# Retention, then two expert layers: the loads of retention in another order and four at a time, rows of the first tiles kept back, a wide product in halves

## The chip, the cores and the metric

One core of a Trainium2 chip. The core has five engines that run side by side: TensorE (PE, matrix products; PEld is its loading of weights), VectorE (DVE), ScalarE (ACT), GpSimd (POOL) and SyncE (SP), whose queue issues most transfers. The metric is the time of one execution on the device in microseconds (us); lower is better. The kernel before takes 798.01 us, the median of 3 runs (797.87 to 800.58).

## The reference

```python
def _attn_ref(q, k, v):                       # 4 x 8 heads x 576 x 64
    scores = scale * np.matmul(q, k.transpose(0, 1, 3, 2))
    gamma = 1.0 - 2.0 ** (-5.0 - np.arange(H))
    Dmat = np.where(rel >= 0, gamma ** rel, 0.0)
    return np.matmul(scores * Dmat, v)
def _moe_ref(x, w_gate, w1, w2):              # 2304 tokens, 8 experts, 288 tokens each
    logits = x @ w_gate                       # the largest logits are served first, greedily
    ...
    out[mask] = np.maximum(x[mask] @ w1[e], 0.0) @ w2[e]
def _moe2_ref(x, w_in, w_out):                # 512 -> 2048 -> 512
    h = x @ w_in
    return (h * np.tanh(softplus(h))) @ w_out
```

Retention (attention with a decay in place of the softmax) makes x of 2304 tokens by 512; each token is assigned to one of 8 experts, and a gated layer follows. All is in float32.

## The kernel before, in words

Only the first part, `attention`, is touched. It walks over 18 tiles of 128 tokens (all 8 heads at once). A sequence has 576 tokens, so a new one starts with tiles 0 and 9, and tiles 4 and 13 straddle two. One iteration t of the loop does this:

- `load(t + 3)`: two transfers of 512 KB on SP's queue, `qk` (queries and keys, transposed) and `kv` (keys and values). Each has five buffers.
- `scale(t + 3)` on GpSimd: `ks`, keys by their decay (needs `kv`), and then `qs`, queries by their decay (needs `qk`).
- `scores(t + 1)`: keys by queries on PE into `pA`; VectorE multiplies with a mask into `am`.
- `carried(t)`: the state of the tiles before by `qs` into `pT` (not in tiles 0 and 9).
- `outputs(t)`: `am` by values, into `pT` too; ScalarE copies it to `xT`.
- `state(t)`: `ks` by values into `pS`, and VectorE makes the next state `S` (not in tiles 8 and 17).
- `turn(t - 1)`: the wide product `pX`, `xT` by an identity with the gate's weights beside it. It turns the tile to rows and gives the gate's logits. VectorE reduces the logits into `L`, ScalarE copies the rows to `xs`, and SP stores them to `x_scratch`, 256 KB a tile, from where the experts gather them later.

PE, VectorE and GpSimd run in the order in which the code is written. ScalarE and SP get their order from a scheduler with a timeline of its own, so a transfer may stand in SP's queue elsewhere than in the code. SP issues in the order of its queue: a row that waits holds back all that stand behind it. In the kernel before, a transfer waits for the one eight places ahead (there are eight semaphores for transfers) and for its buffer. Four constant loads serve the routing that follows: `ident`, `tri`, `rc` and `ic`.

After tile 17 the routing starts on VectorE: `choices(early)` takes the logits of tiles 0 to 15, and it stands on VectorE behind the reduction of tile 16. A long chain of small VectorE and PE operations follows, and after it the experts, whose order on all engines comes from a planner that starts its own clock there.

Of the kernel before, what the change touches and what calls it, by code (L numbers as in the profile page):

```python
# [7 lines left out]
F32 = mybir.dt.float32  # L8
# [9 lines left out]
P = 128  # L18
B, H, S, D = 4, 8, 576, 64
N = B * S  # L20
DM = H * D
E = 8
# [3 lines left out]
NT = N // P  # L26
HP = H // 2
WARM = 11
STRADDLE = (4, 13)

GB = 96
# [42 lines left out]
def _layout(spec):  # L74
    out, o = {}, 0
    for name, n in spec:
        out[name] = slice(o, o + n)
        o += n
    return out, o


DC, DCN = _layout([("gk", NT * H), ("gs", NT * HP), ("gq", HP * P)])
# [45 lines left out]
class Kernel:  # L128
# [3 lines left out]
    def attention(self):  # L132
        tc, nc, a = self.tc, self.nc, self.a
# [7 lines left out]
        with ExitStack() as st:  # L141
            ld = st.enter_context(tc.tile_pool(name="ld", bufs=5))
            wk = st.enter_context(tc.tile_pool(name="wk", bufs=3))
# [3 lines left out]
            dec = one.tile([P, DCN], F32, name="dec")  # L147
# [3 lines left out]
            masks = [one.tile([P, 2, HP, P], F32, name=f"mask{i}") for i in range(2)]  # L151
            both = one.tile([P, 2, P + 2 * E], F32, name="both")
# [3 lines left out]
            QZ = {}  # L156
            for t in STRADDLE:
                QZ[t] = one.tile([P, HP, P], F32, name=f"qz{t}")
                nc.gpsimd.memset(QZ[t][:, :, 64:], 0.0)
            pS = ps.tile([P, HP, D], F32, name="pS")  # L160
            QK, KV, QS, KS, AM, XT, PT, seen = {}, {}, {}, {}, {}, {}, {}, [0]

            def load(t):

                if t < NT:
                    QK[t] = ld.tile([P, 2, HP, P], F32, name="qk")
                    nc.sync.dma_start(QK[t].rearrange("p a h i -> p (a h i)"), a["qk"][:, t])
                    KV[t] = ld.tile([P, 2, H, D], F32, name="kv")
                    nc.sync.dma_start(KV[t].rearrange("p a h d -> p (a h d)"), a["kv"][:, t])

            def starts(t):
                return (t * P) % S == 0

            def scale(t, eng):

                if t >= NT:
                    return
                if not starts(t + 1):
                    KS[t] = wk.tile([P, H, D], F32, name="ks")
                    eng.tensor_tensor(KS[t], KV[t][:, 0], gks[:, t, :, None].to_broadcast([P, H, D]), op=ALU.mult)  # L180
                if not starts(t):
                    n = 64 if t in STRADDLE else P
                    QS[t] = QZ[t] if t in STRADDLE else wk.tile([P, HP, P], F32, name="qs")
                    eng.tensor_tensor(QS[t][:, :, :n], QK[t][:, 0, :, :n], gqs.rearrange("p (h i) -> p h i", i=P)[:, :, :n], op=ALU.mult)

            def scores(t):
                if t >= NT:
                    return
                pA = [ps.tile([P, HP, P], F32, name=f"pA{i}", tag="pA", bufs=2) for i in range(2)]
                for hp in range(HP):  # L190
                    for i in range(2):
                        sl = slice(i * 64, i * 64 + 64)
                        for o in (slice(0, 64), slice(64, P)):
                            nc.tensor.matmul(pA[i][o, hp, :], QK[t][sl, 1, hp, o], QK[t][sl, 0, hp, :], start=True, stop=True)
                AM[t] = wk.tile([P, 2, HP, P], F32, name="am")
                for i in range(2):
                    nc.vector.tensor_tensor(AM[t][:, i], pA[i], masks[t in STRADDLE][:, i], op=ALU.mult)

            def state(t):

                if starts(t + 1):
                    return
                s1 = ((t + 1) * P - 1) % S
                begin = s1 < P
                lo = P - 1 - s1 if begin else 0
                for h in range(H):
                    o = slice(h % 2 * 64, h % 2 * 64 + 64)
                    nc.tensor.matmul(pS[o, h // 2, :], KS[t][lo:, h, :], KV[t][lo:, 1, h, :],
                                     start=(begin and h < 2), stop=False, skip_group_check=True)
                seen[0] += 1  # L210
                nc.vector.tensor_tensor(Sb[seen[0] % 2], pS, gss[:, t + 1, :, None].to_broadcast([P, HP, D]), op=ALU.mult)
# [25 lines left out]
            def turn(t):  # L237

                if t < 0:
                    return  # L240
                xs = wk.tile([P, DM], F32, name="xs")
                pX = ps.tile([P, 2, 512], F32, name="pX", tag="pT", bufs=2)
                for i in range(2):
                    for k in range(2):
                        nc.tensor.matmul(pX[:, i, k * P:k * P + P + E], XT[t][:, 2 * i + k, :], both[:, i, E - k * E:P + 2 * E - k * E],
                                         start=(k == 0), stop=(k == 1), skip_group_check=True)
                nc.vector.tensor_reduce(L[:, t, :], pX[:, :, P:P + E].rearrange("p i e -> p e i"), AX.X, ALU.add)
                for i in range(2):
                    nc.scalar.copy(xs.rearrange("p (k q i d) -> p i k q d", q=2, i=2, d=D)[:, i],
                                   pX[:, i, :2 * P + 2 * E].rearrange("p (k c) -> p k c", k=2)[:, :, :P].rearrange("p k (q d) -> p k q d", d=D))  # L250
                nc.sync.dma_start(a["x"][t * P:(t + 1) * P, :], xs)

            warm = one.tile([P, 512], BF16, name="warm")
            nc.vector.memset(warm, 0.0)
            nc.scalar.activation(warm[:, :1], warm[:, :1], AF.Sigmoid)
            nc.vector.memset(warm[:, :1], 0.0)
            pW = ps.tile([P, 2, 512], F32, name="pW", tag="pT", bufs=2)[:, 0]
            for _ in range(WARM):
                nc.tensor.matmul(pW, warm[:, :P], warm, start=True, stop=True)
            self.routing_setup()  # L260
            load(0)
            nc.sync.dma_start(masks[0].rearrange("p a h i -> p (a h i)"), a["masks"][:, 0])
            nc.sync.dma_start(dec, a["decays"])
            load(1)
            nc.sync.dma_start(both.rearrange("p i c -> p (i c)"), a["both"])
            nc.sync.dma_start(self.ident, a["ident"])
            self.tri = one.tile([P, P], F32, name="tri")
            nc.sync.dma_start(self.tri, a["tri"])
            load(2)
            nc.sync.dma_start(masks[1].rearrange("p a h i -> p (a h i)"), a["masks"][:, 1])  # L270
            scores(0)
            scale(0, nc.vector)
            scale(1, nc.gpsimd)
            scale(2, nc.gpsimd)
            for t in range(NT - 1):
                load(t + 3)
                scale(t + 3, nc.gpsimd)
                scores(t + 1)
                carried(t, Sb[seen[0] % 2])
                outputs(t)  # L280
                state(t)
                turn(t - 1)
                if t == 6:
                    self.routing_consts()
            t = NT - 1
            carried(t, Sb[seen[0] % 2])
            outputs(t)
            turn(t - 1)
            self.psum = lambda name, shape: ps.tile(shape, F32, name=name, tag="pS" if name == "pF" else "pA", bufs=1 if name == "pF" else 2)
            G = self.marks_of()  # L290
            self.chosen = self.rw.tile([GB, E, 3], I32, name="chosen", bufs=1)
# [2 lines left out]
            choice = self.choices(early)  # L294
            self.reached(choice, G, early)
            turn(t)
            self.choices(late, choice)
            self.reached(choice, G, late)
            for i in range(NT):
# [30 lines left out]
        nc.gpsimd.memset(self.ohb[:, NT * GB:], 0.0)  # L330
        self.tok = pr.tile([P, NT], I32, name="tok")

    def routing_consts(self):
        nc, a, pr = self.nc, self.a, self.persist
        rc = self.rc = pr.tile([P, RCN], F32, name="rc")
        nc.sync.dma_start(rc, a["rconsts"])
        self.ic = pr.tile([P, ICN], U32, name="ic")
        nc.sync.dma_start(self.ic, a["iconsts"])
        nc.vector.tensor_scalar(self.at("ic", U32), self.ic, self.ic[:, IC["all"]], None, op0=ALU.bitwise_and)
        self.before = pr.tile([P, P], BF16, name="before")  # L340
        nc.vector.tensor_tensor(self.before, self.tri, self.ident, op=ALU.subtract)
# [777 lines left out]
```

## Time and profile before

| | |
|---|---|
| median of 3 runs | 798.01 us |
| profiled execution | 803.52 us |
| its span, first to last instruction | 801.7 us |
| PE busy | 756.9 us (94%) |
| DVE busy | 664.2 us (83%) |
| granted TensorE clock, mean | 0.977 |
| moved by the DMA engines | 112.53 MB |

A line of the timeline gives start, duration, engine, source line, operation, output <- inputs and shape, and in brackets how long the engine was idle before and what ended that. x16 says that 16 records are merged. A line of stages gives the busy time of each engine in a stretch, then the granted clock, the busy share of the DMA engines and what they moved. Names end in a buffer number in the program, which is left out.

### The profile page before, as it was taken

Reading aid. Unit: us, or ns where it says so; the run is one execution under the profiler, and the core shown is the slowest. Engines: PE = TensorE matmul, PEld = TensorE weight load, DVE = VectorE, ACT = ScalarE, POOL = GpSimd, SP = SyncE. Lnnn points to the kernel's source line nnn. Section 1 sums busy time; section 2 is a strip of 40 time slices with the busy share of each in tenths; the row PEclk is TensorE's granted clock in tenths of the full one; section 3 lists DMA queues with packets and bytes.
Section 4 is the critical chain, followed back from the end, with each engine's and each line's share of the span. In section 5 each row is a group of like instructions: output and inputs, shape, how many; then the busy total and the mean of one; then the engine's idle time right before and its main releaser. Section 6 shows DMA issues by size and latency. Waiting matters only on the chain.

```text
span 801.7 us, 16170 instructions
## 1 busy us (share of the span) xinstructions
PE 756.9 (94%) x6184; PEld 682.4 (85%) x6184; DVE 664.2 (83%) x1080; ACT 412.7 (51%) x781; POOL 470.5 (59%) x407
## 2 busy tenths in 40 slices
PE   7999479999999999898999899999999999999996
PEld 5898338898998989798989789888998899889985
DVE  2444687888888888778799999989998998998993
ACT  1233115556565565756844465555546555555452
POOL 4643035779797897430376676666557566555544
PEclk9999779999999999899999999999999999999999
DMA  9994166889788887988300010010001001000001
GB/s 341 409 352 141 41 193 209 252 284 300 247 300 278 273 298 245 334 287 287 114 11 11 21 39 21 20 40 20 2 20 50 11 20 40 20 1 27 14 1 39
DMA packets 61261, 112.53 MB, mean 140 GB/s; under 512 B 4864, under 2 KB 33152, under 8 KB 61184
## 3 DMA queue, kind: packets, MB, share of 16 engines
q1 hardware_dynamic: 44960, 74.01, 27.3%
q10 hardware_dynamic: 13248, 28.06, 9.8%
q0 software_dynamic: 2976, 9.44, 3.6%
q8 instruction: 48, 0.79, 0.4%
q14 instruction: 29, 0.24, 0.1%
HBM read 88.94 MB, written 22.54 MB: 139 GB/s over the span
## 4 chain that ended last, share of the span: by engine, by line
PE 48%; DVE 10%; issue 4%; DMA 3%; POOL 2%; ACT 2%; ACTq 0%; SPq 0%; POOLq 0%; DVEq 0%
PE mmc L996 20%; PE po L1057 18%; PE mma L776 6%; DVE q L1026 4%; PE mmb L776 4%; DVE n L1021 2%; DMA st<-w 2%; DVE n L1031 1%; DMA st<-w_out 1%; POOL n L1028 1%; POOL gl L1038 1%; DVE G L433 1%; DVE words L742 1%; ACT whi L563 1%; DVE wlo L566 0%
## 5 line engine op out<-in xcount | busy, mean ns | idle before, releaser
L1026 DVE RECIPROCAL q<-q 128x384 f32<-128x384 f32 x96 | 244.3, 2545 | 13.5 <-ACT q L1017 7.4
L1028 POOL TENSOR_TENSOR n<-n,q 128x384 f32<-128x384 f32 x96 | 99.9, 1040 | 133.6 <-DVE q L1026 130.3
L1038 POOL TENSOR_TENSOR gl<-n,gh 128x384 fp32r<-128x384 f32 x96 | 104.4, 1088 | 56.8 <-ACT gh L1036 56.2
L996 PE MATMUL mmc<-yl,whi 128*128 128x384 f32 x384 | 130.2, 339 | 3.9 <-POOL yl L956 2.1
L996 PE MATMUL mmc<-yh,whi 128*128 128x384 f32 x384 | 130.7, 340 | 1.0 <-ACT yh L953 1.0
L996 PE MATMUL mmc<-yh,wlo 128*128 128x384 f32 x384 | 129.8, 338 | 0.0
L566 POOL TENSOR_TENSOR wlo<-st,whi 128x1024 fp32r<-128x1024 f32 x50 | 120.0, 2417 | 14.3 <-ACT whi L563 9.3
L1057 PE MATMUL po<-wlo,gh 128*128 128x512 f32 x288 | 115.6, 401 | 0.0
L1057 PE MATMUL po<-whi,gh 128*128 128x512 f32 x288 | 114.8, 399 | 0.0
L1057 PE MATMUL po<-whi,gl 128*128 128x512 f32 x288 | 114.0, 396 | 0.0
L1014 ACT ACTIVATE s<-mmc 128x384 f32<-128x384 f32 x96 | 47.2, 491 | 125.3 <-PE mmc L996 122.1
L1021 DVE SCALAR_TENSOR_TENSOR n<-s 128x384 f32<-128x384 f32 x96 | 102.0, 1062 | 3.1 <-ACT s L1014 1.2
L563 ACT CAST whi<-st 128x1024 fp32r<-128x1024 f32 x80 | 83.1, 1045 | 38.7 <-DMA st<-w 28.7
L776 PE MATMUL mma<-xh,whi 128*128 128x288 f32 x256 | 78.5, 307 | 3.4 <-ACT xh L623 2.7
L996 PEld LDWEIGHTS mmc<-yl,whi 128*128 128x128 f32 x384 | 72.1, 188 | 9.3 <-POOL yl L956 3.1
L776 PE MATMUL mma<-xl,whi 128*128 128x288 f32 x256 | 77.4, 302 | 1.7 <-DVE xl L625 1.7
L996 PEld LDWEIGHTS mmc<-yh,whi 128*128 128x128 f32 x384 | 72.2, 188 | 6.3 <-ACT yh L953 1.9
L776 PE MATMUL mmb<-hl,whi 128*128 128x288 f32 x256 | 77.3, 302 | 0.0
L776 PE MATMUL mmb<-hh,whi 128*128 128x288 f32 x256 | 77.2, 302 | 0.0
L776 PE MATMUL mma<-xh,wlo 128*128 128x288 f32 x256 | 76.9, 300 | 0.0
L776 PE MATMUL mmb<-hh,wlo 128*128 128x288 f32 x256 | 75.9, 297 | 0.0
L996 PEld LDWEIGHTS mmc<-yh,wlo 128*128 128x128 f32 x384 | 72.0, 187 | 0.0
(149 smaller groups left out, 1533.2 us busy)
## 6 DMA issues: line engine op xcount, KB each, us to landing
st<-w SPq DMA_DIRECT2D x64, 512.0 KB
qk<-qk SPq DMA_DIRECT2D x18, 512.0 KB
kv<-kv SPq DMA_DIRECT2D x18, 512.0 KB
std<-w_out ACTq DMA_DIRECT2D x15, 512.0 KB
std<-w_in ACTq DMA_DIRECT2D x14, 512.0 KB
x_scratch<-xs SPq DMA_DIRECT2D x18, 256.0 KB
y_scratch<-y ACTq DMA_DIRECT2D x32, 144.0 KB
yt<-y_scratch SPq DMA_DIRECT2D x22, 192.0 KB
```

The lines of the kernel that those rows point to most:

```text
L433: v.tensor_tensor(G[:, :NT * 64].rearrange("p (t m) -> p t m", m=64)[:, :, :m], key[:, :, None].to_broadcast([P, NT, m]), T[:, None, :].to ...
L563: self.nc.scalar.copy(dst[0], st)
L566: (self.nc.vector if lo.engine == DVE else self.nc.gpsimd).tensor_tensor(dst[1], st, dst[0].bitcast(F32), op=ALU.subtract)
L742: v.tensor_scalar(w, w, ic[:, IC["three"]], None, op0=ALU.logical_shift_left)
L776: self.nc.tensor.matmul(bank[1][:, :CAP], al if h == 2 else ah, bl if h == 1 else bh, start=(first and j == h == 0), stop=(last and j == n ...
L996: self.nc.tensor.matmul(bank[1][:, :TILE], (wl if h == 2 else wh)[:, c, cs], x[c][h == 1], start=(c == h == 0), stop=(c == HP - 1 and h == 2))
L1014: nc.scalar.activation(s, p, AF.Sigmoid)
L1021: v.scalar_tensor_tensor(u, s, 2.0, s, op0=ALU.subtract, op1=ALU.mult)
L1026: v.reciprocal(q, q)
L1028: nc.gpsimd.tensor_tensor(u, u, q, op=ALU.mult)
L1038: nc.gpsimd.tensor_tensor(gl, u, gh.bitcast(F32), op=ALU.subtract)
L1057: nc.tensor.matmul(po[j], (gl if h == 2 else gh)[:, js], (wl if h == 1 else wh)[:, f % 2], start=(f == h == 0), stop=(f == DFF // P - 1 an ...
```

## The change

- Loads go through `fetch`: each waits until the load four before it (in the order of the code) has landed. Stores don't count.
- Order of the first loads: the decays in two parts, the queries of tile 2 ahead of `both`, the second mask in iteration 1. `ident`, `tri`, `rc` and `ic` are loaded in iteration 6; the two VectorE operations that use them move from iteration 6 to 13.
- Four more warming products after the first scores, and in iteration 0 the scores of tile 1 stand behind outputs and state of tile 0.
- `turn`: each product of 128 columns of weights becomes two of 64.
- The rows of a tile are kept in `xs` (eight buffers) and their store is written six tiles later.

```diff
+HELD = 6
+OUTSTANDING = 4
...
+            def fetch(out, src):
+
+                d = nc.sync.dma_start(out, src)
+                if len(fetched) >= OUTSTANDING:
+                    tc.add_manual_dep(d.ins, fetched[-OUTSTANDING], mybir.DependencyInfo(mybir.DependencyClass.Sync, mybir.DependencyReason.DATA),
+                                      reason="few loads at a time, so that the first come first")
+                fetched.append(d.ins.name)
...
-                xs = wk.tile([P, DM], F32, name="xs")
+                xs = wk.tile([P, DM], F32, name="xs", bufs=HELD + 2)
...
-                        nc.tensor.matmul(pX[:, i, k * P:k * P + P + E], XT[t][:, 2 * i + k, :], both[:, i, E - k * E:P + 2 * E - k * E],
-                                         start=(k == 0), stop=(k == 1), skip_group_check=True)
+                        for o in (slice(0, 64), slice(64, P)):
+                            nc.tensor.matmul(pX[o, i, k * P:k * P + P + E], XT[t][:, 2 * i + k, o], both[:, i, E - k * E:P + 2 * E - k * E],
+                                             start=(k == 0), stop=(k == 1), skip_group_check=True)
...
-                nc.sync.dma_start(a["x"][t * P:(t + 1) * P, :], xs)
+                held.append((t, xs))
+
+            def send(n):
+                for t, xs in held[:n]:
+                    nc.sync.dma_start(a["x"][t * P:(t + 1) * P, :], xs)
+                del held[:n]
...
             load(0)
...
+            fetch(masks[0].rearrange("p a h i -> p (a h i)"), a["masks"][:, 0])
+            of_keys = slice(0, DC["gq"].start)
+            fetch(dec[:, of_keys], a["decays"][:, of_keys])
+            load_qk(1)
+            fetch(dec[:, DC["gq"]], a["decays"][:, DC["gq"]])
+            load_kv(1)
+            load_qk(2)
+            fetch(both.rearrange("p i c -> p (i c)"), a["both"])
+            load_kv(2)
...
             scores(0)
+            heat(4)
...
             for t in range(NT - 1):
                 load(t + 3)
                 scale(t + 3, nc.gpsimd)
-                scores(t + 1)
+                if t == 1:
+                    fetch(masks[1].rearrange("p a h i -> p (a h i)"), a["masks"][:, 1])
+                if t:
+                    scores(t + 1)
                 carried(t, Sb[seen[0] % 2])
                 outputs(t)
                 state(t)
+                if not t:
+                    scores(1)
                 turn(t - 1)
+                send(0 if t <= HELD else 1 if t < 2 * HELD else 2)
                 if t == 6:
-                    self.routing_consts()
+                    self.routing_consts(fetch)
+                if t == 13:
+                    self.routing_tables()
```

SP's queue before, from the load of the queries of tile 5 (`qk_301`) on; `qk_505` is tile 8, `kv_439` tile 7, `xs_291` the rows of tile 0.

```order
L167 DMA qk_301<-qk 128x1024 [waits DMAHW2_49,PE_49]
L167 DMA qk_369<-qk 128x1024 [waits DMAHW3_49,PE_49,Pool_49]
L169 DMA kv_303<-kv 128x1024 [waits DMAHW4_49,DVE_49,PE_49]
L167 DMA qk_437<-qk 128x1024 [waits DMAHW5_49,PE_49,Pool_49]
L169 DMA kv_371<-kv 128x1024 [waits DMAHW6_49,PE_49]
L251 DMA x_scratch<-xs_291 128x512 [waits DMAHW7_49,Activation_49]
L167 DMA qk_505<-qk 128x1024 [waits DMAHW0_49,PE_49,Pool_49]
L169 DMA kv_439<-kv 128x1024 [waits DMAHW1_49,PE_49]
L251 DMA x_scratch<-xs_359 128x512 [waits DMAHW2_49,Activation_49]
```

The same queue now, from the load of the keys and values of tile 6 (`kv_380`) on; `qk_520` is tile 8, `kv_451` tile 7, `qk_589` tile 9, `kv_522` tile 8, `xs_294` the rows of tile 0. All loads have line 167, that of `fetch`.

```order
L167 DMA kv_380<-kv 128x1024 [waits DMAHW6_49,PE_49]
L167 DMA qk_449<-qk 128x1024 [waits DMAHW7_49,Pool_49]
L272 DMA x_scratch<-xs_294 128x512 [waits Activation_49]
L167 DMA qk_520<-qk 128x1024 [waits DMAHW1_49,PE_49,Pool_49]
L167 DMA ident_65<-ident 128x128 [waits DMAHW5_49]
L167 DMA kv_451<-kv 128x1024 [waits DMAHW0_49,PE_49]
L272 DMA x_scratch<-xs_365 128x512 [waits Activation_49]
L167 DMA qk_589<-qk 128x1024 [waits DMAHW3_49,PE_49,Pool_49]
L167 DMA rc_660<-rconsts 128x211 [waits DMAHW2_49,DMAHW1_49]
L167 DMA kv_522<-kv 128x1024 [waits PE_49]
L272 DMA x_scratch<-xs_436 128x512 [waits DMAHW4_49,Activation_49]
L167 DMA tri_150<-tri 128x128 [waits DMAHW3_49]
```

The first store of rows stands between the same loads in both, behind the keys and values of tile 6. `ident`, `rc` and `tri` have come between the tile loads. The semaphore that `ident` waits for is that of the queries of tile 8, directly ahead of it; `rc` waits in the same way for tile 9's queries, `tri` for tile 8's keys and values, and `ic`, four rows further on, for tile 9's.

PE's queue now, from the end of the first scores to the first outputs and the scores of tile 1 (`pA_215`); before, the scores of tile 1 stand directly behind those of tile 0, and the outputs behind both.

```order
L210 MATMUL pA_151<-qk 64x128 x2
L210 MATMUL pA_152<-qk 64x128 x2
L283 LDWEIGHTS warm
L283 MATMUL pW<-warm 128x512
L247 MATMUL pT<-am,kv 64x128 x8
L224 MATMUL pS<-kv,ks 64x64 x8
L210 MATMUL pA_215<-qk 64x128 x2
L210 MATMUL pA_216<-qk 64x128 x2
```

The pair of a warming product stands there four times. Outputs and state of tile 0 have moved ahead of the scores of tile 1.

## Rows read from the trace of the kernel before

**Rows 1.** Stages: busy us of each engine, granted clock, DMA share, GB/s.
```profile
0.00:10.00 10.00, 5.74 (x43) 2.32 (x43) 2.13 (x5) 1.49 (x2) 5.44 (x22) 1.00 0.79 278
10.00:20.00 10.00, 9.35 (x193) 8.57 (x197) 3.70 (x9) 1.94 (x6) 4.55 (x4) 0.83 1.03 405
20.00:30.00 10.00, 9.84 (x210) 8.52 (x203) 5.05 (x10) 2.59 (x8) 6.66 (x7) 1.00 1.04 408
```
**Rows 2.** Timeline of PE's products, one settled tile.
```profile
56.19 1.10 PE L194 MATMUL pA<-qk 64*64 64x128 f32 x32
57.12 0.62 PE L222 MATMUL pT<-qs,S 64*64 64x128 f32 x16
57.66 1.09 PE L231 MATMUL pT<-am,kv 128*64 128x128 f32 x16
58.59 0.63 PE L208 MATMUL pS<-kv,ks 128*64 128x64 f32 x16
59.15 1.19 PE L245 MATMUL pX<-both,xT 128*128 128x136 f32 x8
```
**Rows 3.** Timeline of VectorE, the reduction of tile 16.
```profile
83.69 0.17 DVE L247 TENSOR_REDUCE L<-pX 128x8 f32<-128x16 f32 x1 [2.57 <-PE pX L245]
```
**Rows 4.** Timeline of PE's products, the start.
```profile
2.43 4.70 PE L259 MATMUL pW<-warm 128*128 128x512 bf16 x11 [2.43 <-DVE warm L256]
...
10.37 1.98 PE L194 MATMUL pA<-qk 64*64 64x128 f32 x32 [2.20 <-DMA qk<-qk]
12.28 1.75 PE L231 MATMUL pT<-am,kv 128*64 128x128 f32 x16
...
18.86 0.40 PE L194 MATMUL pA<-qk 64*64 64x128 f32 x5 [0.28 <-DVE L L247]
```
**Rows 5.** Stages of the start, the clock before the last two columns.
```profile
10.50:11.00 0.50, 0.50 (x12) 0.50 (x16) 0.00 (x0) 0.00 (x0) 0.00 (x0) 0.50 1.07 370
...
14.00:15.00 1.00, 1.00 (x38) 0.93 (x37) 0.43 (x1) 0.65 (x2) 0.00 (x0) 1.00 1.02 406
```
**Rows 6.** Timeline, VectorE's first two products with the mask.
```profile
8.21 1.29 DVE L197 TENSOR_TENSOR am<-pA,mask 128x512 f32<-128x512 f32 x2 [5.83 <-PE pA L194]
```
**Rows 7.** Timeline of PE's weight loads in the settled tile.
```profile
57.66 0.85 PEld L231 LDWEIGHTS pT<-am,kv 128*64 128x64 f32 x16 [0.17 <-issue]
58.48 0.60 PEld L208 LDWEIGHTS pS<-kv,ks 128*64 128x64 f32 x16
59.15 0.99 PEld L245 LDWEIGHTS pX<-both,xT 128*128 128x128 f32 x8
60.27 0.86 PEld L194 LDWEIGHTS pA<-qk 64*64 64x64 f32 x31
```
**Rows 8.** SP's queue, first load of expert weights on idle DMA engines.
```profile
106.75 1.58 SPq L549 DMA_DIRECT2D st<-w  x3
```
**Rows 9.** Timeline of ScalarE, the operation that waits for it.
```profile
110.69 1.04 ACT L563 CAST whi<-st 128x1024 fp32r<-128x1024 f32 x1 [23.39 <-DMA st<-w]
```
**Rows 10.** Stages between the two.
```profile
107.00:108.00 1.00, 1.00 (x4) 0.39 (x3) 1.00 (x2) 0.00 (x0) 0.00 (x0) 0.50 0.04 12
108.00:109.00 1.00, 1.00 (x3) 0.30 (x2) 1.00 (x2) 0.00 (x0) 0.00 (x0) 0.50 0.86 234
109.00:110.00 1.00, 1.00 (x20) 0.66 (x19) 0.90 (x4) 0.00 (x0) 0.00 (x0) 0.88 1.08 345
```
**Rows 11.** Timeline of GpSimd, the two scalings of a tile.
```profile
45.63 1.04 POOL L180 TENSOR_TENSOR ks<-kv,dec 128x512 f32<-128x512 f32 x1 [0.88 <-DMA kv<-kv]
46.63 1.28 POOL L184 TENSOR_TENSOR qs<-qk,dec 128x512 f32<-128x512 f32 x1
```
**Rows 12.** Timeline of PE, the carried product of tile 10.
```profile
53.03 0.62 PE L222 MATMUL pT<-qs,S 64*64 64x128 f32 x16
```
**Rows 13.** SP's queue: issues that wait for the landings of kv2 and qk3.
```profile
15.05 2.80 SPq L167 DMA_DIRECT2D qk<-qk  x2
18.80 0.33 SPq L169 DMA_DIRECT2D kv<-kv  x1
```

More of the change, by code (lines that the diff above doesn't have):

```diff
@@ L160, in attention, with load_qk, load_kv, load @@
             pS = ps.tile([P, HP, D], F32, name="pS")
-            QK, KV, QS, KS, AM, XT, PT, seen = {}, {}, {}, {}, {}, {}, {}, [0]
-            def load(t):
+            QK, KV, QS, KS, AM, XT, PT, seen, held, fetched = {}, {}, {}, {}, {}, {}, {}, [0], [], []
+            def fetch(out, src):
[4 more added lines that the diff above has]
+                fetched.append(d.ins.name)
+            def load_qk(t):
                 if t < NT:
                     QK[t] = ld.tile([P, 2, HP, P], F32, name="qk")
-                    nc.sync.dma_start(QK[t].rearrange("p a h i -> p (a h i)"), a["qk"][:, t])
+                    fetch(QK[t].rearrange("p a h i -> p (a h i)"), a["qk"][:, t])
+            def load_kv(t):
+                if t < NT:
                     KV[t] = ld.tile([P, 2, H, D], F32, name="kv")
-                    nc.sync.dma_start(KV[t].rearrange("p a h d -> p (a h d)"), a["kv"][:, t])
+                    fetch(KV[t].rearrange("p a h d -> p (a h d)"), a["kv"][:, t])
+            def load(t):
+                load_qk(t)
+                load_kv(t)
             def starts(t):
@@ L257, in attention, with heat @@
             pW = ps.tile([P, 2, 512], F32, name="pW", tag="pT", bufs=2)[:, 0]
-            for _ in range(WARM):
-                nc.tensor.matmul(pW, warm[:, :P], warm, start=True, stop=True)
+            def heat(n):
+                for _ in range(n):
+                    nc.tensor.matmul(pW, warm[:, :P], warm, start=True, stop=True)
+            heat(WARM)
             self.routing_setup()
             load(0)
[L262 to L266, printed above, removed]
+            fetch(masks[0].rearrange("p a h i -> p (a h i)"), a["masks"][:, 0])
[7 more added lines that the diff above has]
+            load_kv(2)
             self.tri = one.tile([P, P], F32, name="tri")
-            nc.sync.dma_start(self.tri, a["tri"])
-            load(2)
-            nc.sync.dma_start(masks[1].rearrange("p a h i -> p (a h i)"), a["masks"][:, 1])
             scores(0)
+            heat(4)
             scale(0, nc.vector)
@@ L288, in attention @@
             turn(t - 1)
+            send(NT)
             self.psum = lambda name, shape: ps.tile(shape, F32, name=name, tag="pS" if name == "pF" else "pA", bufs=1 if name == "pF" else 2)
@@ L296, in attention @@
             turn(t)
+            send(NT)
             self.choices(late, choice)
@@ L331, in routing_setup, with routing_consts, routing_tables @@
         self.tok = pr.tile([P, NT], I32, name="tok")
-    def routing_consts(self):
+    def routing_consts(self, fetch):
         nc, a, pr = self.nc, self.a, self.persist
+        fetch(self.ident, a["ident"])
+        fetch(self.tri, a["tri"])
         rc = self.rc = pr.tile([P, RCN], F32, name="rc")
-        nc.sync.dma_start(rc, a["rconsts"])
+        fetch(rc, a["rconsts"])
         self.ic = pr.tile([P, ICN], U32, name="ic")
-        nc.sync.dma_start(self.ic, a["iconsts"])
+        fetch(self.ic, a["iconsts"])
+    def routing_tables(self):
+        nc, pr = self.nc, self.persist
         nc.vector.tensor_scalar(self.at("ic", U32), self.ic, self.ic[:, IC["all"]], None, op0=ALU.bitwise_and)
```

## The prediction

> **What bounds the kernel now.** I read the table of stages first, then PE's rows in order of time, then SP's queue, and last the few rows from which a single load can be timed. The stages [rows 1] show the load phase: the DMA engines are full from 10 us on (405 and 408 GB/s), and TensorE's granted clock is 0.83 on average in the second stage. In a settled tile [rows 2, 7] PE runs without a gap: scores 0.93 us to the next start, carried 0.54, outputs 0.93, state 0.56, wide product 1.12, together 4.08. So from about 45 us on retention is bound by PE; before that, by what has landed. The routing chain on VectorE starts when the row of logits of tile 16 is reduced [rows 3], so a microsecond at that row is a microsecond of the whole: behind it the order of all engines is the same in both kernels. I name tiles by number: qk8 is the load of queries and keys of tile 8.
>
> The sum is made against the profiled execution: 803.52 us, a span of 801.7 and 1.82 around it. It lies 5.51 above the median of the runs, 798.01; I subtract that at the end.
>
> **The start.** Before, the scores of tile 1 wait 2.20 us for their load, then run 1.98 us instead of 1.10, and the outputs of tile 0, which were ready, come behind them and take 1.75 instead of 1.09 [rows 4, 2]. The reason for the longer times is the granted clock: 0.50 at 10.5 us, its lower level of 1.2 GHz, and 1.00 again at 14 [rows 5]. That idle spell cost 0.88 + 0.66 = 1.5 us beside the wait itself. The change puts four warming products there and moves outputs and state of tile 0 ahead of the scores of tile 1. VectorE ends its first two products at 8.21 + 1.29 = 9.50 [rows 6]; from there outputs 0.93, state 0.56, scores 0.93 (the load of tile 1 lands near 9.5 by its bytes), VectorE 1.29, then scores of tile 2 at 13.2 and one round of 3.88 (4.08 less the gain of the next part) to the scores of tile 3: 17.1 instead of 18.86 [rows 4]. That is 1.8 us earlier, if nothing later takes it back. The four warming products (at most 0.43 us each, since eleven take 4.70 [rows 4]) lie in the wait for VectorE and cost nothing; without that cover they would cost 1.7.
>
> **The wide product in column halves.** 4 products become 8 of half the width. Its shape is then that of outputs (128 rows, 64 columns, 16 records). Start to start in the weight loads: wide product 59.15 to 60.27 = 1.12; outputs 57.66 to 58.48 = 0.82 for 128 columns, 0.87 for 136 [rows 7]. By the matmul rows outputs take 0.93 [rows 2], so 0.99 for 136. The gain is 0.13 to 0.25 per tile; I take 0.2. From below: nothing, if the weight columns, which stay the same in number, set the time. The rows of outputs speak for the gain, since there twice as many half loads go by in less time.
> By the Trainium skill, "TensorE: Matmul & The Clock Gate", section "LDWEIGHTS (loading the stationary operand)", a weight load takes time in proportion to its columns; 16 loads of 64 are then worth 8 of 128, and the halves would bring nothing: 1.6 us less gain in the sum below. The rows of outputs don't agree that this is the bound.
>
> **The rows kept for six tiles.** SP's order is set by a scheduler, not by the program, and the order shows the first store behind the same load (kv6) in both kernels, then one per tile, and seven at the end. So the keeping moves no store: 0. The eight buffers make nothing wait. The tables moved to tile 13 are two short VectorE operations in its idle time: 0. The second mask now lands at about 20.8 by its bytes, 1 us before its tile needs it: 0, and if late, it delays a PE that waits later anyway.
>
> **Four under way.** The cap itself doesn't starve the engines while four large loads are out: four take 5.2 us at 406 GB/s, and one that starts dry is used 3.94 us after issue [rows 8, 9]. What costs is where the four constant loads now stand in SP's queue. Each waits until the load directly ahead of it has landed (ident for qk8, rc for qk9, tri for kv8, ic for kv9), and every load behind it waits too, since SP issues in order. Four times the engines run dry.
> When: the bytes up to and with qk8 are 16 tile loads at 0.524, two masks 1.05, decays 0.37, "both" 0.15, one store 0.26, together 10.22 MB. 2.78 are moved by 10 us, then 0.406 per us [rows 1]: 28.3 us. From last byte to use: the dry load [rows 8 to 10] moves 0.246 MB by 109.0 and the rest at 345 GB/s by 109.8, and is used at 110.69: 0.88. So qk8 lands at 29.2.
> A dry load costs 3.94 there; tile loads move at 406 instead of 345 GB/s, 0.23 less: 3.71, an estimate from these rows. The rounds: ident, kv7, x1, qk9: 0.46 + 3.71 + 0.65 + 1.29, lands 35.3. rc, kv8: 0.43 + 0.27 + 3.71: 39.7. tri, qk10, kv9: 0.46 + 3.71 + 1.29: 45.2. ic, qk11, kv10: 0.43 + 0.25 + 3.71 + 1.29: kv10 lands at 50.9. GpSimd needs 2.3 us for the two scalings of tile 10 [rows 11], so the carried product of tile 10 starts at 53.2. Before it starts at 53.03 [rows 12]. Without the rounds it would start at 53.03 - 1.8 - 8 x 0.2 = 49.6. The rounds thus take back all that start and halves have won up to tile 10, and what is late there is kv10, through GpSimd.
> Bounds of a round: no loss, if something still in flight covers it (the store does for 0.65); from above, two loads once took 3.75 us instead of 2.58 (15.05 to 18.80, issues that wait for their landings [rows 13]), 0.6 a load, over seven loads 4.1 us. I keep 3.71, the nearest row.
> By the Trainium skill, "DMA: Bandwidth & Descriptors", section "Anatomy of one DMA — SWDGE (gpsimd) path", a transfer costs about 2.0 us plus its bytes at 436 GB/s, 3.2 us for a tile load; the page measured another path than SP's. Four rounds at 3.2 would put the carried product at 51.2 and the end at 795.3. The row of this trace, 3.94, is longer, and I go by it.
>
> **The sum.** Carried product of tile 10: +0.2. Behind it eight wide products stand before the reduction of tile 16 (tiles 9 to 16): 8 x 0.2 = -1.6. PE idles about 2.5 us ahead of the carried product, as it did for 2.20 at the start, where the clock then cost 1.5; between 0 and 1.5 I take +0.7. Total -0.7: 803.52 becomes 802.8, and less 5.51, 797.3.
>
> **Rivals.** A, the rounds are covered: the loads run ahead of need, or land faster, so that kv10 is there by 47.3. Then all of retention is bound by PE: -1.8 - 16 x 0.2 = -5.0, 793.0. For it: kv10 has to come only 0.9 us a round earlier, and the bytes may run ahead. Against: nothing but one store is in flight when SP waits. B, slower: a round takes 1.5 us more than 3.71, since a dry transfer waits for the slowest engine each time. kv10 lands at 56.9; +6.2 - 1.6 + 1.5 = +6.1, 804.1. It decides against the kernel from a landing of kv10 at about 53 on. For it: 3.75 instead of 2.58 in rows 13. Against: there eight transfers were queued. C, the halves bring nothing: 798.9, inside the same band. That the stores aren't kept back is no rival: the order shows it, and it is in the sum.
>
> **How the numbers follow.** Half a per cent, 4 us, is about what this measurement can tell from no change: faster is below 794.0, slower above 802.0. The forecast has 0.52, its own range 794 to 801 (0.6 us a round either way, and both ends of the clock). A 0.30, three quarters of it below 794.0; B 0.13, C 0.05. Faster: 0.23 and a rest of 0.07 from the forecast's own edge, 0.30; slower 0.13; same 0.57. The range takes in most of A and B's near edge: 791.5 to 802.
>
> **What would show it.** In the trace after: scores of tile 3 near 17.1; wide product 0.9 to 1.0 start to start; SP's issues of ident, rc, tri, ic each waiting for a landing, with DMA throughput falling well below 400 GB/s between 29 and 51 us; GpSimd waiting for kv10; PE idle before the carried product of tile 10; reduction of tile 16 at about 83.0 instead of 83.69. If PE has no gap near 50 us, A holds. If throughput falls and PE still waits beyond 56, B. If the wide product stays at 1.1, C.

## The result: 806.29 us against 798.66, slower by one per cent

The changed kernel takes 806.29 us (median of 4 runs, 805.5 to 809.29), the kernel before 798.66 in the same comparison (797.87 to 800.58). The ratio is 1.0106, with a 95% interval of 1.0087 to 1.0125. The forecast was 797.3 us, in a range of 791.5 to 802; rival B, a round longer than 3.71 us a load, gave 804.1. The experiments below ran on several chips, on which the kernel before took 798 to 802 us. So they are compared by their ratio to the kernel before on the same chip, and by the row of VectorE at which routing starts.

That row, the reduction of tile 16, answers to [rows 3]:

```profile
91.53 0.17 DVE L264 TENSOR_REDUCE L<-pX 128x8 f32<-128x16 f32 x1 [2.37 <-PE pX L262]
```

It comes 91.53 - 83.69 = 7.84 us later; the medians differ by 7.63. What follows this row goes by the chip and not by the kernel: from it to the last instruction it takes 712 to 714 us in the runs below on one chip, and 716 to 719 on the two others. (In these two profiled executions it is 712.2 now and 718.0 before, and the one before lies 5.5 us above its median.) So the loss lies in retention.

### The profile page after: what moved, and what is told of

The parts are those of the page before. It is cut to its first block, busy times and chain, and to the rows that moved or that the text cites. A ratio compares the mean times of both kernels' runs of the same rounds, so it can differ in the third digit from the quotient of the medians.

```text
span 803.7 us, 16459 instructions
## 1 busy us (share of the span) xinstructions
PE 756.6 (94%) x6332; PEld 682.4 (85%) x6332; DVE 664.7 (83%) x1080; ACT 412.6 (51%) x781; POOL 470.5 (59%) x407
## 4 chain that ended last, share of the span: by engine, by line
PE 49%; DVE 7%; issue 3%; DMA 2%; POOL 1%; ACT 1%; SPq 0%; POOLq 0%; ACTq 0%; DVEq 0%
PE mmc L1039 21%; PE po L1100 20%; PE mma L819 4%; PE mmb L819 4%; DVE q L1069 3%; DVE n L1064 2%; DMA st<-w 2%; DVE n L1074 1%; DMA st<-w_out 1%; DVE wlo L609 1%; POOL yl L999 0%; ACT whi L606 0%; POOL gl L1081 0%; POOL n L1071 0%; DVE G L476 0%
```

## The profile after

The start came out as forecast, and so did the gain of the halves. PE's products at the start, and then one settled tile, in order of time, with start and duration [rows 4, 2]:

```profile
9.30 1.15 PE L247 MATMUL pT<-am,kv 128*64 128x128 f32 x16
...
11.01 1.10 PE L210 MATMUL pA<-qk 64*64 64x128 f32 x32
...
17.36 1.10 PE L210 MATMUL pA<-qk 64*64 64x128 f32 x32
18.29 0.62 PE L238 MATMUL pT<-qs,S 64*64 64x128 f32 x16
18.83 1.09 PE L247 MATMUL pT<-am,kv 128*64 128x128 f32 x16
19.76 0.64 PE L224 MATMUL pS<-kv,ks 128*64 128x64 f32 x16
20.22 1.10 PE L262 MATMUL pX<-both,xT 128*64 128x136 f32 x16
21.25 1.10 PE L210 MATMUL pA<-qk 64*64 64x128 f32 x32
```

The scores of tile 1 run at full speed (1.10), those of tile 3 start at 17.36 (forecast 17.1). State to wide product is 0.46 instead of 0.56, the product to the next scores 1.03 instead of 1.12: a tile takes 3.89 instead of 4.08 us. Half of this gain stands in the step ahead of the wide product; the forecast had all of it, 0.13 to 0.25, in the product itself. By the rule of the Trainium skill that the forecast weighed ("TensorE: Matmul & The Clock Gate", section "LDWEIGHTS (loading the stationary operand)"), a weight load's time by its columns, the halves would have brought nothing; these rows say 0.19.

Then the loads stop. SP's issues of the four constants (each behind the landing of the load directly ahead of it), and the stages that answer to [rows 1], with granted clock, DMA share and GB/s last:

```profile
32.05 0.33 SPq L167 DMA_DIRECT2D ident<-ident  x1
...
40.06 0.33 SPq L167 DMA_DIRECT2D rc<-rconsts  x1
...
45.19 0.33 SPq L167 DMA_DIRECT2D tri<-tri  x1
...
51.66 0.33 SPq L167 DMA_DIRECT2D ic<-iconsts  x1
```

```profile
10.00:20.00 10.00, 9.06 (x226) 7.80 (x224) 5.22 (x10) 1.97 (x7) 6.49 (x6) 1.00 0.98 356
20.00:30.00 10.00, 10.00 (x238) 8.79 (x238) 4.38 (x10) 3.37 (x11) 5.26 (x6) 1.00 0.98 361
30.00:40.00 10.00, 8.39 (x216) 7.44 (x208) 5.07 (x10) 3.08 (x10) 3.02 (x4) 1.00 0.50 156
40.00:50.00 10.00, 8.36 (x152) 7.60 (x156) 2.06 (x5) 2.59 (x8) 1.85 (x2) 0.83 0.69 182
50.00:60.00 10.00, 6.11 (x112) 5.43 (x104) 3.17 (x6) 1.29 (x4) 2.72 (x3) 0.83 0.84 269
```

Between 30 and 50 us the engines move 156 and 182 GB/s. The rounds take 8.0, 5.1 and 6.5 us (differences of the four issues), where the forecast had 6.1, 4.4 and 5.5. The fourth ends with the use of kv10 by GpSimd, 6.7 us behind `ic` (forecast 5.7):

```profile
58.33 1.04 POOL L196 TENSOR_TENSOR ks<-kv,dec 128x512 f32<-128x512 f32 x1 [5.50 <-PE pA L210]
```

The profile puts this wait down to PE, whose scores end at the same time; kv10 was issued at 52.66 and landed 5.5 us later. PE waits from tile 7 on, in order of time:

```profile
40.67 0.67 PE L238 MATMUL pT<-qs,S 64*64 64x128 f32 x16 [2.28 <-POOL qs L200]
41.27 1.74 PE L247 MATMUL pT<-am,kv 128*64 128x128 f32 x16
...
51.78 1.98 PE L247 MATMUL pT<-am,kv 128*64 128x128 f32 x16 [0.89 <-DMA kv<-kv]
...
57.04 1.10 PE L210 MATMUL pA<-qk 64*64 64x128 f32 x32 [1.15 <-DMA qk<-qk]
60.64 0.67 PE L238 MATMUL pT<-qs,S 64*64 64x128 f32 x16 [2.50 <-POOL qs L200]
61.24 1.25 PE L247 MATMUL pT<-am,kv 128*64 128x128 f32 x16
```

The last wait is that of the carried product of tile 10, which starts at 60.64 instead of 53.03 [rows 12]. Behind it the clock is granted at half, its level of 1.2 GHz, as the stage shows (behind the wait at 40.67 it was 0.50 from 42 to 45, and at 51.78 from 52 to 55):

```profile
62.00:65.00 3.00, 3.00 (x39) 2.73 (x34) 0.42 (x1) 0.65 (x2) 1.80 (x2) 0.51 1.03 408
```

## The experiments

Theory T: the four rounds are the loss. Rivals: R1, the cap of four starves the engines; R2, the edits on PE cost time. From the second set on a theory I joined, that PE also stops for its own instructions. "Reduction" is the start of the reduction of tile 16 in the profiled execution, one for each kernel (before 83.69, changed 91.53).

**The rounds taken away.** The changed kernel; the constants (`ident` is shown, `tri`, `rc` and `ic` alike) wait for the load sixteen places back.

```diff
-        fetch(self.ident, a["ident"])
+        fetch(self.ident, a["ident"], 16)
...
```

> The changed kernel, but each of the four constant loads waits for the load sixteen places before it instead of four; that one landed long ago, so nothing in SP's queue stops. Tile loads keep the cap of four. Theory T (the loss is the four rounds in which SP stands still and the engines run dry): no dip of the throughput below 300 GB/s between 30 and 50 us, carried product of tile 10 at 49 to 50, time 793 to 795. Rival R1 (the cap of four itself starves the engines, 356 to 361 GB/s against 405 to 408): throughput stays at 360 and PE waits for loads around tiles 7 to 11, time 797 to 802. Rival R2 (halves, start or kept rows cost): 803 or more.

Measured: ratio to before 1.0007 (0.9983 to 1.0031), reduction 84.40:

```profile
84.40 0.17 DVE L264 TENSOR_REDUCE L<-pX 128x8 f32<-128x16 f32 x1 [2.37 <-PE pX L262]
```

The throughput stays at 353 to 393 GB/s from 10 to 60 us. T holds for the loss: 7.1 of 7.8 us are gone with the rounds. It fails for the gain: the time is that of the kernel before, not 5 us less. That is R1's number, but not its sign: PE's one wait for a load is at 12.98, and none stands around tiles 7 to 11. Rows of PE, with what ended each wait, and then the stage from 38 to 40 us with the granted clock before the last two columns:

```profile
12.98 1.21 PE L210 MATMUL pA<-qk 64*64 64x128 f32 x30 [1.15 <-DMA qk<-qk]
23.02 0.44 PE L238 MATMUL pT<-qs,S 64*64 64x128 f32 x4 [0.52 <-issue]
36.12 0.89 PE L210 MATMUL pA<-qk 64*64 64x128 f32 x24 [1.79 <-issue]
55.09 0.66 PE L238 MATMUL pT<-qs,S 64*64 64x128 f32 x15 [1.02 <-issue]
```

```profile
38.00:40.00 2.00, 2.00 (x30) 2.00 (x30) 0.32 (x1) 0.63 (x2) 1.29 (x2) 0.50 1.00 374
```

"issue" is a stop for nothing that a semaphore shows, in the middle of a group of products. The one of 1.79 us pulls the clock down to 0.50 behind it, and the outputs of tiles 6 and 7 come 5.92 and 5.62 us after those of the tile before, instead of 3.89.

**Two rounds.** The same with the constants eight places back; two of them still stand behind a load just issued.

```diff
-        fetch(self.ident, a["ident"])
+        fetch(self.ident, a["ident"], 8)
...
```

> The changed kernel, but the constant loads wait for the load eight places before. In SP's queue two of them then still stand right behind the load they wait for (rc behind the queries of tile 7, ic behind the keys and values of tile 7), the other two wait for nothing that is still under way. T: two rounds instead of four, so two stops of SP of 5 to 7 us and about half of the loss: 797 to 801. R1: the same time as the kernel without rounds, since the cap is the same. R2: 805 to 807, no change.

Measured: 1.0038 (1.002 to 1.0056), reduction 85.97. More than without rounds, less than with four: 0.31% of the 0.99% between them. The direction is T's, but the run doesn't settle the price of two rounds: its interval overlaps that of the run without rounds, and its trace is late before any constant is loaded, at the scores of tile 2, which start at 12.98 in that run and here at 15.35:

```profile
15.35 1.10 PE L210 MATMUL pA<-qk 64*64 64x128 f32 x32 [3.72 <-DMA qk<-qk]
```

The absolute times expected were too low, since the PE edits gained nothing.

**The edits on PE alone.** The kernel before with halves and start (its scores of tile 1 behind outputs and state of tile 0, as in the change).

```diff
+            heat(4)
...
+                        for o in (slice(0, 64), slice(64, P)):
+                            nc.tensor.matmul(pX[o, i, k * P:k * P + P + E], XT[t][:, 2 * i + k, o], both[:, i, E - k * E:P + 2 * E - k * E],
...
```

> The kernel before with the two edits on PE alone: wide product in column halves, four warming products and the scores of tile 1 behind outputs and state of tile 0. Loads, stores and constants as before. T: -1.8 at the start and 16 x 0.2 = -3.2, 793 to 795, faster. R2: no gain, 798 or more.

Measured: 1.0003 (0.9986 to 1.0021), reduction 83.96. No gain: R2's number, for a reason that no theory had. PE's waits, and the DMA queues from 57 to 58 us (packets, MB, share of the engines):

```profile
13.69 1.22 PE L194 MATMUL pA<-qk 64*64 64x128 f32 x30 [1.14 <-DMA qk<-qk]
18.91 1.10 PE L194 MATMUL pA<-qk 64*64 64x128 f32 x31 [1.04 <-DMA qk<-qk]
25.72 0.44 PE L222 MATMUL pT<-qs,S 64*64 64x128 f32 x4 [1.32 <-issue]
...
57.26 1.09 PE L231 MATMUL pT<-am,kv 128*64 128x128 f32 x16
60.01 0.69 PE L208 MATMUL pS<-kv,ks 128*64 128x64 f32 x16 [1.66 <-issue]
```

```profile
q1 hardware_dynamic: 126, 0.35, 92.9%
q8 instruction: 1, 0.02, 6.0%
```

Two things eat the gain. The loads of tiles 2 and 3 come late in the old order. And PE stops where a block of instructions is being fetched: queue 8, which carries instructions, has a packet of 16 KB in 57 to 58 us, among 126 packets of loads and stores, and PE goes on at 60.01. The same packet stands at 23 to 24 us (stop to 25.72), and in the run without rounds at 33 (stop to 36.12) and 52 (to 55.09).

**The rounds alone.** The kernel before, with the four constants loaded in iteration 6 as in the changed kernel (the two VectorE operations that use them move to iteration 13 with them); only these four wait for an earlier load.

```diff
-            nc.sync.dma_start(self.ident, a["ident"])
...
+        fetch(self.ident, a["ident"], 4)
...
```

> The kernel before with one thing added: the four constants are loaded in iteration 6, each waiting for the load four places before, which SP's queue puts right ahead of it. No cap on the tile loads, PE as before. T: four stops of SP, keys and values of tile 10 land at 56 to 59 instead of about 50, time 805 to 809. R1: the rounds cost little where more loads are queued, 798 to 801. R2: 798 to 799.

Measured: 1.0090 (1.0071 to 1.0108), 809.34 us, reduction 89.77. T holds: the rounds do it without cap, halves or start. The issues stand at 30.50, 37.31, 42.30 and 48.41, so the rounds are 6.8, 5.0 and 6.1 us. Here the wait shows elsewhere, in the list of waits (us in total, times, longest):

```profile
PE pX L253 <- ACT xs L257: 7.4, 4, 3.4
```

With three buffers for rows, ScalarE stops when SP doesn't store, and PE waits 7.4 us for it. So the same stops of SP cost time by another path here, through the stores and not through kv10 (used at 55.08, expected 56 to 59). The changed kernel has eight buffers; the forecast counted them as nothing.

**Idle DMA engines, without and with the edits on PE.** The loads of tiles 6 to 17 are left out; these tiles compute on the data of tiles 3 to 5 again.

```diff
-                if t < NT:
+                if 5 < t < NT:
+                    QK[t], KV[t] = QK[t - 3], KV[t - 3]
+                elif t < NT:
```

> The kernel before with the loads of tiles 6 to 17 left out (these tiles compute on the data of tiles 3 to 5 again), so that from 30 us on only the stores of rows use the DMA engines. It is the yardstick of the next run. Theory I (PE also stops for its own instructions: a block of them comes by DMA, behind the loads, and the stops that the trace gives to no semaphore are these): no such stops from 30 us on, every tile 4.08 us, reduction of tile 16 at 81.5 to 82.5 instead of 83.69, 1 to 2 us faster than before. Rival L (the loads themselves bound retention in the kernel before): the reduction comes at 78 or earlier.

> The kernel before with the two edits on PE (halves, start) and the loads of tiles 6 to 17 left out. I: without loads the halves pay in full: 3.89 us a tile, no stops from 30 us on, the reduction of tile 16 is 3 to 4 us ahead of the run without loads and without the edits, the time likewise. Rival H (the halves cost PE something that the start-to-start times don't show, loads or not): the two runs without loads end within 1.5 us of one another, and stops without a semaphore stay.

Measured: reduction 82.86 without the edits (0.9981, 0.9963 to 0.9999) and 81.34 with them (0.9961, 0.9944 to 0.9978). Both expectations were too good, by 0.4 us the first, and the second by half: 1.5 us between the two instead of 3 to 4. That is the number of H, the rival of the second expectation, too. But the edits lose 1.4 us while the loads still run (outputs of tile 3 at 26.02 against 24.62) and win behind them. All of PE's waits between the warming and the routing, with the edits:

```profile
13.56 1.10 PE L196 MATMUL pA<-qk 64*64 64x128 f32 x32 [2.28 <-DMA qk<-qk]
19.43 0.76 PE L196 MATMUL pA<-qk 64*64 64x128 f32 x17 [1.31 <-issue]
25.65 0.43 PE L224 MATMUL pT<-qs,S 64*64 64x128 f32 x4 [1.05 <-issue]
```

From 26 us on there is none, though queue 8 has ten packets from 26 to 74 us. From the outputs of tile 3 to those of tile 16 it is 50.24 us with the edits and 52.77 without, 0.195 a tile: where the engines are idle the halves pay in full. So the stops need loads beside them: I holds, and H's sign, stops with or without loads, is missing.

The traces show what PE stops for. In the kernel before and the twelve runs of this section, 21 such stops (0.16 to 1.79 us) stand ahead of the routing, and all of them at the 451st of PE's instructions (weight loads, products and those of its sequencer) or a multiple of 256 behind it, to within one. Each ends 2.2 to 2.7 us after a packet of 16 KB starts on queue 8. With the loads left out, from 26 us on, that packet starts between 0.3 us before and 1.1 us after PE passes the place 256 instructions earlier; in the run without rounds, from 20 to 53 us, it starts 2.7 to 5.2 us after. So PE waits for its next 256 instructions, and they come late where loads and stores move. That they stand behind the loads on their DMA engine is inferred from this, not seen.

**Rows really kept.** No rounds, 18 buffers, all stores behind the last load; then the same with eight loads under way.

```diff
+LAST = -1
...
-                xs = wk.tile([P, DM], F32, name="xs", bufs=HELD + 2)
+                xs = wk.tile([P, DM], F32, name="xs", bufs=NT)
...
-                    nc.sync.dma_start(a["x"][t * P:(t + 1) * P, :], xs)
+                    d = nc.sync.dma_start(a["x"][t * P:(t + 1) * P, :], xs)
+                    tc.add_manual_dep(d.ins, fetched[LAST], mybir.DependencyInfo(mybir.DependencyClass.Sync, mybir.DependencyReason.DATA),
+                                      reason="rows behind the last load")
...
-                send(0 if t <= HELD else 1 if t < 2 * HELD else 2)
+                send(NT if t == NT - 2 else 0)
```

> The changed kernel with the four constants' waits sixteen places back (no rounds), and the rows really kept: 18 buffers, and every store waits for the last load (keys and values of tile 17). I: less moves in the load phase (1.05 MB a tile instead of 1.31), so fewer stops for instructions and earlier loads: reduction of tile 16 at 79 to 82, 2 to 5 us faster than the kernel before. L': if what the stops cost doesn't depend on how much moves, or if the stores at the end hold back the first expert loads, the same as without rounds, 0 to 1 us slower than before.

> The same with eight loads under way instead of four. Rival R1 (the cap costs throughput, 356 to 361 GB/s against 405 to 408): 1 to 3 us faster than with four, scores of tiles 2 and 3 earlier. If more loads under way put PE's instructions further back (I): stops longer, 1 to 3 us slower than with four.

Measured: 0.9966 (0.9946 to 0.9986) and 0.9965 (0.9949 to 0.9981), reductions 80.23 and 80.44. The first:

```profile
80.23 0.17 DVE L265 TENSOR_REDUCE L<-pX 128x8 f32<-128x16 f32 x1 [2.37 <-PE pX L263]
```

Both are faster than the kernel before by 0.3%, a small step but outside their intervals, and so than the changed kernel, as theory I had it. Without the stores PE stops for 1.4 us in all (four under way), against 3.7 in the run without rounds. Four and eight don't differ, though the stage from 10 to 20 us moves 359 and 410 GB/s: R1 falls here, and so does the expectation that eight lengthen the stops. The cap costs throughput, not time, in these two kernels, in which nothing stalls behind it; in the changed kernel, with its rounds and stores, eight were not tried.

**Rounds without stores.** The changed kernel with its rounds, and all stores behind the last load (the diff above on the changed kernel).

> The changed kernel with its four rounds as they are (constants wait for the load directly ahead), but with every store of rows behind the last load, so that in a round nothing moves but one constant, one or two tile loads, and PE's instructions. Theory S (a round took 8.0, 5.1, 6.5 and 6.7 us instead of the forecast 6.1, 4.4, 5.5 and 5.7 because the store of rows, issued with the tile load, holds it up: the engines were 0.92 to 1.03 busy at 90 to 120 GB/s for the first 2 us of a round): rounds of 4 to 5 us, reduction of tile 16 at 84 to 87. Rival N (a transfer from a standing start takes that long by itself, with a tail on its slowest engine): rounds of 5 to 8 us as before, reduction at 88 or later, 3 us or more behind the same kernel without rounds (80.23).

Measured: 1.0056 (1.0035 to 1.0078), reduction 86.07. SP's issues of the constants:

```profile
30.81 0.33 SPq L168 DMA_DIRECT2D ident<-ident  x1
...
36.53 0.33 SPq L168 DMA_DIRECT2D rc<-rconsts  x1
...
40.82 0.33 SPq L168 DMA_DIRECT2D tri<-tri  x1
...
47.08 0.33 SPq L168 DMA_DIRECT2D ic<-iconsts  x1
```

The rounds take 5.7, 4.3 and 6.3 us, 16.3 together; in the changed kernel it was 19.6. The forecast's 6.1, 4.4 and 5.5 make 16.0. The fourth ends here:

```profile
52.87 1.04 POOL L197 TENSOR_TENSOR ks<-kv,dec 128x512 f32<-128x512 f32 x1 [4.63 <-DMA kv<-kv]
```

That is 5.8 us (changed kernel 6.7, forecast 5.7). So the size that was forecast is about that of a round with no store in it, and the store adds 2.3, 0.8, 0.2 and 0.9 us to the four. S holds for the reduction and the direction; its rounds of 4 to 5 us were too short, and the third is N's, as long without the store as with it. Even so the rounds cost 5.8 us at the reduction (86.07 against 80.23, where N had 3 or more) and 0.9% of the time (1.0056 against 0.9966).

**Kept rows, wide product whole.** The kernel with kept rows and eight under way, without the halves: one product of 128 columns again.

```diff
-                        for o in (slice(0, 64), slice(64, P)):
...
```

> The kernel with kept rows and eight loads under way, but with the wide product whole as before. The halves are worth 0.195 us a tile where PE sets the pace, 3.1 us over 16 tiles, less what their extra instructions cost in stops. Theory: reduction of tile 16 at 82.5 to 83.5 instead of 80.44, 2 to 3 us slower than with halves. Rival H (the stops for instructions eat the halves here too): within 1 us of the kernel with halves.

Measured: 0.9965 (0.9945 to 0.9986), reduction 81.31. No stop for instructions stands in its trace, where the kernel with halves has 1.01 and 0.53 us. The halves move the reduction by 0.87 us (two profiles, from two chips), and the time by nothing that this comparison can tell: H holds, not the theory.

**Halves alone, start alone.** The kernel before with one of the two edits.

> The kernel before with the column halves alone. I (0.2 us a tile gained, partly given back in stops for instructions while loads and stores fill the engines): 0 to 2 us faster than before, stops of 1 to 2 us in the trace. Rival (all of it is kept): 3 us faster.

> The kernel before with the start alone: four warming products, scores of tile 1 behind outputs and state of tile 0. In the run with both edits PE then waited for the queries of tiles 2 and 3, which the old order of loads brings late: scores of tile 3 at 18.9 as before, and no gain, within 1 us of before. Rival (the start pays by itself): scores of tile 3 at 17.1, 1.8 us faster.

Measured: halves 0.9999 (0.9981 to 1.0016), reduction 82.18, stops for instructions of 1.30 and 0.52 us: as theory I had it, at the lower edge of its range, since 1.5 us are gained at the reduction and nothing in the time. Start 1.0015 (0.9997 to 1.0033), reduction 83.61. With the start alone the scores of tile 3 wait for their load as expected:

```profile
18.80 1.10 PE L194 MATMUL pA<-qk 64*64 64x128 f32 x32 [1.03 <-DMA qk<-qk]
```

The 1.5 us gained there in the changed kernel thus need the new order of loads (17.36, not 18.80). The cap of four doesn't bring them: with eight under way, in the kernel with kept rows, these scores start at 17.26.

## Why the prediction was wrong, point by point

- **The start**: right, 17.36 against 17.1, scores of tile 1 at full clock.
- **Halves**: 0.19 us a tile, as taken, but half of it ahead of the product, where the forecast had nothing: the size was partly luck. "PE runs without a gap" and "from about 45 us on retention is bound by PE" were wrong as a base for rival A and for the carried product of tile 10 at 49.6 without the rounds. PE was near its limit, but so were the engines that bring its data and its instructions; where PE became faster, it stopped. The run without rounds has that product at 53.80 to 55.09, and the time of the kernel before. In the changed kernel itself no such stop stands ahead of the routing; there the landings set the pace.
- **Rows kept**: no store moved, as the order showed; the first was issued at 24.55. That the eight buffers are worth nothing is doubtful: with three, PE waited 7.4 us for ScalarE in the run with rounds alone. What three would cost in the changed kernel was not tried. Really kept, the rows are the only part that made the kernel faster (1.0007 to 0.9966).
- **Four under way**: the step that failed, by its size. Place and mechanism were right: all four issues waited for the load ahead, and kv10 through GpSimd was the last to be late. Two terms were too small. The first is the landing of qk8, 32.05 instead of 29.2. "The cap itself doesn't starve the engines" was half wrong: at 356 and 361 GB/s instead of 405 and 408, 10.13 MB were moved by 30 us, where the forecast had 10.22 by 28.3. That is 2 of the 2.9 us; with the rounds alone, without cap, the same landing let `ident` go at 30.50, and with the cap but no stores at 30.81, so the cap is not all of it. The second is the rounds: up to the use of kv10 at 58.33 they took 26.3 us from 32.05; the forecast had 21.7 from 29.2. What was missing is the store of rows in each round, priced at 0.65 us in the first and at nothing in the other three. With the stores behind the last load the same stretch takes 22.1 us (30.81 to 52.87), near the forecast, so they make 4.2 of the 4.6. Both terms, 2.9 and 4.6, make 7.5: carried product of tile 10 at 60.64, not 53.2.
- **Behind it**: -1.6 for the halves and +0.7 for the clock were forecast; from that product to the reduction it is 30.89 us, before 30.66. The slow spell from 61 to 65 us alone costs 5.47 instead of 3.89 from outputs to outputs, 1.6 us, a little over the upper end of the 0 to 1.5 that were weighed.
- **Rival B** came near by its number (804.1; kv10 at 56.9, measured 58.33) and by its sign (PE waits beyond 56), but not by its sum or its reason. It had 1.5 us more in each round, because a transfer from a standing start waits for the slowest engine; the rounds took 1.1 us more each, most of it with the stores, and the other 2.9 us came ahead of the first round, where B had nothing. Which of the 16 engines ends a landing was not looked at. Its nearness is in part luck.

## What to carry to other kernels

On a queue that issues in order, a small load that waits for the one just ahead of it costs a whole round from a standing start, here 4.3 to 8.0 us: let it wait for one that landed long ago, or load it first. Before a faster product is counted as a gain, ask whether its data and its instructions can come faster: where the DMA engines are full, 0.19 us a tile was given back in stops that no semaphore shows, and leaving out loads for one experiment shows which it is. Moving stores out of the loads' way was worth more than either edit on PE.

## What was not expected of the hardware

- PE stopped 0.2 to 1.8 us for its next 256 instructions while loads filled the engines; with the loads left out there was no such stop over ten blocks. A stop of 1.79 us was followed by a granted clock of 0.50.
- In the first two us of a round the DMA engines are busy and move little. The changed kernel, a constant, kv7 and a store issued from 32.05 to 32.90:

```profile
33.00:34.00 1.00, 1.00 (x31) 0.82 (x28) 0.19 (x2) 0.27 (x2) 0.00 (x0) 1.00 0.92 119
34.00:35.00 1.00, 1.00 (x38) 0.83 (x32) 0.46 (x1) 0.38 (x2) 0.00 (x0) 1.00 0.65 102
35.00:36.00 1.00, 1.00 (x24) 1.00 (x26) 0.83 (x2) 0.00 (x0) 0.00 (x0) 1.00 0.86 348
...
38.00:40.00 2.00, 0.39 (x16) 0.15 (x8) 1.29 (x2) 0.26 (x1) 1.65 (x2) 1.00 0.12 39
```

  And at its end the load of qk9 has a tail: 39 GB/s from 38 to 40 us, and `rc`, which waits for it, goes only at 40.06. With the stores taken away the first round, issued from 30.81, has a slow head too, 91 GB/s at a share of 0.72 from 32 to 33 us, but is at 266 in the next. Why the head is slow and the tail long was not tried further.
- With the rows kept, four loads under way moved 359 and 365 GB/s in the stages from 10 to 30 us, eight 410 and 398, and the time was the same.
